# Where the attention output of a unit is summed: over the unit's q tile in place of its product buffer

## The chip, the cores and the metric

The kernel runs on one NeuronCore of a Trainium2 chip. The metric is the device time in microseconds (us) of one launch. Engines are named as in the profile: PE (TensorE, matrix products; PEld its weight loads), DVE (VectorE), ACT (ScalarE), POOL (GpSimd) and SP (SyncE, which here only issues DMAs). DMAs are issued from SP, ACT and POOL.

## The reference, cut to what matters

```python
xn = layernorm(x)                            # x: 2048 x 640, float32
q, k, v = split(xn @ wqkv)                   # 32 heads of 20
logits[s, w] = q[s] . k[s - 2*w] * 20**-0.5  # w = 0..7: a window of 8 rows, two apart; masked if s - 2*w < 0
o[s] = sum_w softmax(logits)[s, w] * v[s - 2*w]
s = o @ wo
h = (xn @ w_gate) * (xn @ w_up)              # 640 -> 1536
out = x + s * silu(h @ w_down)
```

## The kernel before

All matrix products are float32 work done as three products of high and low parts (`mm3` and `ALL3`), so a result tile of 512 columns takes 15 PE instructions. The work on PE has one order, written out by hand:

1. The rows are normalised and transposed.
2. Ten *units* follow. A unit is a group of 5, 6 or 7 heads (`GROUPS`) for the even or the odd rows (`DIL` = 2). Unit numbers 0, 2, 4, ... hold the even rows, 1, 3, 5, ... the odd ones. For each unit, `qkv(u, i)` computes eight row tiles (i = 0 to 7) in PE, each into one of four PSUM buffers with the tag `q`. ACT copies each result out: L317 the k and v part into the `kv` buffer of that parity (there is one for even and one for odd units), L318 the q part into the unit's q tile in SBUF (tag `q`, two buffers: unit u + 2 takes the buffer of unit u). L322 then shifts k and v by one partition with DMAs from ACT's queue, for the window.
3. Between units, PE computes four *pieces* of the feed-forward part (`gate_up`): a g product and a u product, each into one of two PSUM buffers (tags `g` and `u`). ACT copies g to SBUF (L423, `gs`), and DVE multiplies it with u (L434, `hs`). That frees the u buffer for the piece after the next.
4. The attention of a unit runs on DVE, as a generator (`attention(u)`) that `advance` moves on by a budget while PE works at the next unit or its pieces. So DVE's one queue holds the attention instructions with the L434s of the pieces between them. The order of each queue is fixed when the program is built.
5. After the units come the output projection and the down projection, which PE does without attention beside it.

Inside `attention(u)` a *pair tile* holds two of the eight window places, 2 x 800 to 2 x 1120 elements per partition. Pair tiles have the tag `t` and two buffers, which they take in turn: the products q times k (L351, `times`), their sums over the 20 elements of a head (L355, `total`), the exponential on ACT (L367), then the products of weights and v (L376) in one pair tile, `t`, added up into the other, `acc` (L384). Last, L387 adds the two halves of `acc`, and L392 stores the sum from SP to the scratch tensor `o_scr` in DRAM, in one DMA or two. The unit uses six pair tiles, an even number, so the second pair tile of the next unit's attention (the `times(2)` of L351) takes the buffer that was `acc`.

```python
for act, j in ((times, 0), (times, 2), (total, 0), (times, 4), (total, 2), (times, 6), (total, 4), (total, 6)):
```

Of the kernel before, what the change touches and what calls it, by code (L numbers as in the profile page):

```python
# [50 lines left out]
def kernel(  # L51
# [11 lines left out]
    nc = tc.nc  # L63
# [11 lines left out]
    def st(shape, tag, bufs, dt=F32):  # L75
        cnt[0] += 1
        return sb.tile(shape, dt, tag=tag, bufs=bufs, name=f"{tag}_{cnt[0]}")
# [248 lines left out]
    def attention(u):  # L326
        g, r = UN[u]
        nh = GROUPS[g]
        c = nh * DH
        q, kv = q_t[u], kv_t[u]  # L330
        pair, one, small = [(n + 155) / 950 for n in (2 * NE * c, NE * c, NE * nh * W)]
        lg = st([P, NE * nh, W], "lg", 2)
        e = lg
        yield 1.0

        def places(a, j):

            y = kv[:, a, j:j + NE, :].rearrange("p i c -> p (i c)")
            return bass.AP(y.tensor, y.offset, [y.ap[0], [c, 2], y.ap[1]])

        def pair_tile():
            return st([P, 2, NE * c], "t", 2)

        def heads(y):
            return y.rearrange("p a (n d) -> p a n d", d=DH)

        prods = {}

        def times(j):
            prods[j] = pair_tile()  # L350
            nc.vector.tensor_mul(prods[j], q.rearrange("p i c -> p (i c)").unsqueeze(1).to_broadcast([P, 2, NE * c]),  # L351
                                 places(0, j))

        def total(j):
            nc.vector.tensor_reduce(out=lg[:, :, j:j + 2].rearrange("p n a -> p a n"), in_=heads(prods.pop(j)),  # L355
                                    op=ALU.add, axis=AX.X)

        for act, j in ((times, 0), (times, 2), (total, 0), (times, 4), (total, 2), (times, 6), (total, 4), (total, 6)):
            act(j)
            yield pair  # L360
        m0 = lg[0:1].rearrange("p (i h) w -> p i h w", h=nh)
        nc.vector.tensor_add(m0, m0, mask.unsqueeze(2).to_broadcast([1, NE, nh, W]))
        sm = st([P, 2, NE * nh], "sm", 2)
        nc.vector.tensor_reduce(out=sm[:, 0, :], in_=lg, op=ALU.max, axis=AX.X)
        nc.vector.tensor_sub(lg, lg, sm[:, 0, :].unsqueeze(2).to_broadcast([P, NE * nh, W]))
        yield 3 * small
        nc.scalar.activation(e, lg, AF.Exp, scale=SCALE)  # L367
        yield small
        nc.vector.tensor_reduce(out=sm[:, 0, :], in_=e, op=ALU.add, axis=AX.X)
        nc.vector.reciprocal(sm[:, 1, :], sm[:, 0, :])  # L370
        nc.vector.tensor_mul(e, e, sm[:, 1, :].unsqueeze(2).to_broadcast([P, NE * nh, W]))
        yield 3 * small

        def weighted(j, t):
            pw = e[:, :, j:j + 2].rearrange("p n a -> p a n").unsqueeze(3).to_broadcast([P, 2, NE * nh, DH])
            nc.vector.tensor_mul(heads(t), pw, heads(places(1, j)))  # L376

        t, acc = pair_tile(), pair_tile()
        weighted(PAIRS[0], acc)
        yield pair  # L380
        for j in PAIRS[1:]:
            weighted(j, t)
            yield pair
            nc.vector.tensor_add(acc, acc, t)  # L384
            yield pair
        o = acc[:, 0, :].rearrange("p (i c) -> p i c", c=c)
        nc.vector.tensor_add(acc[:, 0, :], acc[:, 0, :], acc[:, 1, :])  # L387
        yield one
        for b in range(NQ):
            c0, c1 = max(GOFF[g], b * QC), min(GOFF[g] + c, (b + 1) * QC)  # L390
            if c0 < c1:
                nc.sync.dma_start(o_scr[r, b, :, :, c0 - b * QC:c1 - b * QC].rearrange("s p c -> p s c"),  # L392
                                  o[:, :, c0 - GOFF[g]:c1 - GOFF[g]])
# [328 lines left out]
    for i in range(8):  # L722
        if i == 3:
            running.append((0, attention(0)))
        if i == 2:
            load_wq(1, ((0, 3), (3, 5)))
            low_parts()
        if i < 2:
            trans_odd(14 + i)
        qkv(1, i)  # L730
        advance(PACE * 1.9)
    running.append((1, attention(1)))
    split_wq(1, nc.gpsimd)
    gate_up(0, 2)
# [19 lines left out]
    def unit(u):  # L754
        drain(u - 2)
        begin_unit(u)
        for i in range(NE):
            if u % 2 and u + 1 < len(UN) and i == 2:
                load_wq(UN[u + 1][0], ((0, 3), (3, 5)))
            qkv(u, i)  # L760
            if i == 1:
                finish_piece()
            advance(PACE * GROUPS[UN[u][0]] * 0.38)
        running.append((u, attention(u)))
        if u % 2 and u + 1 < len(UN):
            split_wq(UN[u + 1][0], nc.gpsimd)
# [127 lines left out]
```

## Time and profile before

| | |
|---|---|
| median of 3 runs | 778.89 us (778.88 to 779.15) |
| the profiled execution | 778.73 us, span of the trace 776.7 us |
| PE busy | 765.1 us, 99% of the span |
| DVE busy | 622.9 us, 80% |
| ACT busy | 250.9 us, 32% |
| POOL busy | 103.4 us, 13% |
| waits of DVE for the store to `o_scr`, at L351 | 18.9 us in 7 waits |
| waits of DVE for the shift of k and v, at L351 | 18.5 us in 6 waits |
| from issue to landing, 16 DMAs of L392 | 3.8 us least, 4.9 median, 8.8 most |

Busy time is the time in which an engine has an instruction of its own running. A row of a timeline gives start, duration, engine, line, operation, output and inputs (partitions x elements), and behind it in brackets how long the engine stood still before and what ended that. `xc`, `wf`, `wqh` and `wql` are the transposed rows and the weights; `lg` holds logits and weights of the window.

### The profile page before, as it was taken

The numbers are of one execution on the slowest core, as the hardware profiler recorded it, in microseconds if no ns is written. First come the engines' busy times: TensorE is split into PE (matmuls) and PEld (weight loads), VectorE is DVE, ScalarE is ACT, GpSimd is POOL, SyncE is SP. The second block draws the span as 40 slices with busy tenths as digits, with TensorE's granted clock in tenths as the row PEclk, the third lists the DMA queues.
The fourth block names the chain that finished last, engine by engine and source line by source line (L and its number), as shares of the span: only waits on it lengthen the run. The fifth ranks groups of instructions, "written<-read, shape, count | busy, mean of one in ns | idle before, by whom it ended". The sixth has DMA issues, their size and how long they took to land.

```text
span 776.7 us, 10632 instructions
## 1 busy us (share of the span) xinstructions
PE 765.1 (99%) x4214; PEld 704.9 (91%) x4214; DVE 622.9 (80%) x615; ACT 250.9 (32%) x519; POOL 103.4 (13%) x111
## 2 busy tenths in 40 slices
PE   8999999999899999999999999999999999999997
PEld 6989898897898989989889898888999999999997
DVE  6889889995989989699898898990277577777775
ACT  5333422132112241122412122112366554444442
POOL 5301110101001010000100000004387500000000
PEclk9999999999999999999999999999999999999999
DMA  9172441447133371433732413452897474555533
GB/s 330 62 233 84 90 117 45 96 147 129 34 93 87 113 169 47 104 86 111 147 71 80 111 31 112 109 159 75 190 270 211 160 265 169 193 188 184 183 103 136
DMA packets 82277, 103.33 MB, mean 133 GB/s; under 512 B 19036, under 2 KB 61376, under 8 KB 82100
## 3 DMA queue, kind: packets, MB, share of 16 engines
q1 hardware_dynamic: 72400, 82.85, 34.1%
q0 software_dynamic: 4128, 10.70, 8.3%
q10 hardware_dynamic: 5700, 9.11, 4.2%
q8 instruction: 33, 0.54, 0.3%
q14 instruction: 16, 0.13, 0.1%
HBM read 65.23 MB, written 28.31 MB: 120 GB/s over the span
## 4 chain that ended last, share of the span: by engine, by line
PE 83%; DVE 10%; DMA 4%; issue 2%; ACT 1%; SPq 0%; POOL 0%; DVEq 0%; POOLq 0%; ACTq 0%
PE q L315 21%; PE u L101 17%; PE g L101 16%; PE q L632 11%; PE q L101 9%; PE u L632 5%; PE g L632 3%; DVE t L376 3%; DVE lg L355 2%; DMA o_scr<-t 2%; DVE t L384 2%; DMA wraw<-in_wgu 1%; DVE t L351 1%; DVE hs L434 1%; DMA wraw<-in_wqkv 0%
## 5 line engine op out<-in xcount | busy, mean ns | idle before, releaser
L101 PE MATMUL u<-xc,wf 128*128 128x512 f32 (+1 forms) x735 | 173.5, 388 | 4.1 <-DVE hs L434 4.1
L101 PE MATMUL g<-xc,wf 128*128 128x512 f32 (+1 forms) x735 | 171.7, 385 | 0.0
L101 PEld LDWEIGHTS u<-xc,wf 128*128 128x128 f32 x735 | 137.1, 189 | 32.3 <-DVE hs L434 4.5
L101 PEld LDWEIGHTS g<-xc,wf 128*128 128x128 f32 x735 | 135.9, 188 | 26.6
L315 PE MATMUL q<-wqh,xc 128*128 128x420 f32 (+2 forms) x800 | 153.0, 334 | 1.6 <-ACT xc L244 0.9
L315 PEld LDWEIGHTS q<-wqh,xc 128*128 128x128 f32 x800 | 138.9, 188 | 3.4 <-ACT xc L244 1.3
L351 DVE TENSOR_TENSOR t<-q,kv 128x2240 f32<-128x2240 f32 (+2 forms) x40 | 91.2, 2287 | 37.6 <-DMA o_scr<-t 18.9
L376 DVE TENSOR_TENSOR t<-lg,kv 128x2240 f32<-128x2240 f32 (+2 forms) x40 | 90.8, 2290 | 0.9
L355 DVE TENSOR_REDUCE lg<-t 128x112 f32<-128x2240 f32 (+2 forms) x40 | 90.4, 2280 | 0.0
L423 ACT ACTIVATE gs<-g 128x512 f32<-128x512 f32 x48 | 28.6, 596 | 174.1 <-PE g L101 149.1
L315 PE MATMUL q<-wql,xc 128*128 128x420 f32 (+2 forms) x400 | 81.8, 334 | 0.0
L317 ACT ACTIVATE kv<-q 128x280 f32<-128x280 f32 (+2 forms) x80 | 30.6, 383 | 135.7 <-PE q L315 132.2
L315 PEld LDWEIGHTS q<-wql,xc 128*128 128x128 f32 x400 | 69.9, 188 | 0.0
L384 DVE TENSOR_TENSOR t<-t,t 128x2240 f32<-128x2240 f32 (+2 forms) x30 | 68.7, 2289 | 0.8
L632 PE MATMUL q<-xc,wf 128*128 128x320 f32 x432 | 67.3, 309 | 0.0
L632 PEld LDWEIGHTS q<-xc,wf 128*128 128x128 f32 x432 | 64.3, 188 | 0.0
L92 POOL DMA_DIRECT2D wf<-in_wgu x10 | 8.7, 873 | 283.9 <-ACT wf L91 277.9
L101 PE MATMUL q<-wf,wf 128*128 128x320 f32 x156 | 35.5, 309 | 0.0
L92 POOL DMA_DIRECT2D wql<-in_wqkv x8 | 10.2, 1281 | 131.6 <-ACT wql L91 131.0
L101 PEld LDWEIGHTS q<-wf,wf 128*128 128x128 f32 x156 | 26.1, 188 | 0.0
L434 DVE TENSOR_TENSOR hs<-u,gs 128x512 f32<-128x512 f32 x38 | 25.9, 682 | 0.0
L86 DVE TENSOR_TENSOR wf<-ot,wf 128x640 fp32r<-128x640 f32 x13 | 14.0, 1078 | 12.8 <-ACT wf L85 12.8
(167 smaller groups left out, 919.6 us busy)
## 6 DMA issues: line engine op xcount, KB each, us to landing
h_scr<-hs SPq DMA_DIRECT2D x48, 256.0 KB, 2.2
wraw<-in_wgu SPq DMA_DIRECT2D x12, 640.0 KB, 7.0
wf<-in_wgu POOLq DMA_DIRECT2D x10, 640.0 KB, 6.7
t<-h_scr SPq DMA_DIRECT2D x8, 768.0 KB, 7.1
hs<-s_scr SPq DMA_DIRECT2D x16, 320.0 KB, 4.3
gs<-in_x SPq DMA_DIRECT2D x16, 320.0 KB, 4.8
wraw<-h_scr SPq DMA_DIRECT2D x12, 384.0 KB, 6.3
out<-q SPq DMA_DIRECT2D x14, 320.0 KB, 3.8
```

The costliest lines, as they stand in the source:

```text
L86: eng.tensor_sub(lo, raw, hi.bitcast(F32))
L92: nc.gpsimd.dma_start(lo, src, accum_op=ALU.add)
L101: nc.tensor.matmul(acc, a, b, start=first and n == 0, stop=last and n == len(runs) - 1)
L315: nc.tensor.matmul(p, xT[(r * NE + i) // TPC][a][:, k, t0:t0 + P], wq[g][b][:, k], start=n == 0, stop=n == len(runs) - 1, skip_group_check ...
L317: nc.scalar.activation(kv_t[u][:, :, W - 1 + i, :], p[:, c:].rearrange("p (a c) -> p a c", a=2), AF.Copy)
L351: nc.vector.tensor_mul(prods[j], q.rearrange("p i c -> p (i c)").unsqueeze(1).to_broadcast([P, 2, NE * c]), places(0, j))
L355: nc.vector.tensor_reduce(out=lg[:, :, j:j + 2].rearrange("p n a -> p a n"), in_=heads(prods.pop(j)), op=ALU.add, axis=AX.X)
L376: nc.vector.tensor_mul(heads(t), pw, heads(places(1, j)))
L384: nc.vector.tensor_add(acc, acc, t)
L423: nc.scalar.activation(gs, pp[0], AF.Copy)
L434: nc.vector.tensor_mul(hs, pp[1], gs)
L632: nc.tensor.matmul(p, y[:, i, k], wd_t[name][k][:, l], start=new and r == 0, stop=r == len(runs) - 1, skip_group_check=True)
```

## The change

The last half-sum of a unit (L387) no longer overwrites the first half of `acc`; it is written over the unit's q tile, which the unit's attention has by then read for the last time (in `times(6)`). The store L392 reads it from there. Nothing else is edited.

```diff
-        o = acc[:, 0, :].rearrange("p (i c) -> p i c", c=c)
-        nc.vector.tensor_add(acc[:, 0, :], acc[:, 0, :], acc[:, 1, :])
+        o = q
+        nc.vector.tensor_add(o.rearrange("p i c -> p (i c)"), acc[:, 0, :], acc[:, 1, :])
         yield one
         for b in range(NQ):
             c0, c1 = max(GOFF[g], b * QC), min(GOFF[g] + c, (b + 1) * QC)
             if c0 < c1:
                 nc.sync.dma_start(o_scr[r, b, :, :, c0 - b * QC:c1 - b * QC].rearrange("s p c -> p s c"),
                                   o[:, :, c0 - GOFF[g]:c1 - GOFF[g]])
```

No engine's instructions change their number or their order. What changes is the waits, which the program's framework works out from who writes and reads each buffer.

On DVE, at the end of unit 2's attention and the start of unit 3's (`t_1584` is unit 2's `acc`, `q_1127` unit 2's q, `q_1472` unit 3's q; `DMAHW6` and the like count landings of DMAs on one of eight lanes):

```order
 L384 TENSOR_TENSOR t_1584<-t_1584,t_1583 128x1920 [waits DVE_49]
-L387 TENSOR_TENSOR t_1584<-t_1584 128x960 [waits DVE_49]
+L387 TENSOR_TENSOR q_1127<-t_1584 128x960 [waits DMAHW6_49,DVE_49]
 L434 TENSOR_TENSOR hs_1717<-u_1657,gs_1673 128x512 [waits DMAHW0_49,PE_49,Activation_49]
 L351 TENSOR_TENSOR t_1723<-q_1472,kv_109_763 128x1920 [waits DMAHW6_49,DMAHW5_49,DMAHW7_49,DMAHW0_49,Pool_49]
-L351 TENSOR_TENSOR t_1740<-q_1472,kv_109_763 128x1920 [waits DMAHW3_49,DMAHW2_49,DVE_49]
+L351 TENSOR_TENSOR t_1740<-q_1472,kv_109_763 128x1920 [waits DVE_49]
 L355 TENSOR_REDUCE lg_1722<-t_1723 128x2x48 [waits DVE_49]
 L434 TENSOR_TENSOR hs_1762<-u_1694,gs_1710 128x512 [waits DMAHW1_49,PE_49,Activation_49]
```

The second L351 of unit 3 no longer waits for the two DMAs of unit 2's store (lanes 2 and 3). The wait that L387 now names is for unit 0's store, from the buffer that unit 2's q later took.

On ACT, at the first row tile of unit 2, whose q takes the buffer of unit 0's q (`q_1129` and `q_1149` are PSUM results of PE, `q_1127` is the tile in SBUF):

```order
 L423 ACTIVATE gs_1101<-g_1084 128x512 [waits DVE_49,PE_49,Activation_49]
 L317 ACTIVATE kv_38_169<-q_1129 128x2x120 [waits DMAHW3_49,DMAHW4_49,DVE_49,PE_49]
-L318 ACTIVATE q_1127<-q_1129 128x120
+L318 ACTIVATE q_1127<-q_1129 128x120 [waits DMAHW6_49,DVE_49]
 L317 ACTIVATE kv_38_169<-q_1149 128x2x120 [waits PE_49]
 L318 ACTIVATE q_1127<-q_1149 128x120
```

The first L318 of a unit now waits for L387 and for the landing of the store two units before.

## The prediction

> **What bounds the kernel now.** I read the page's first part, then the waits of PE, the timeline of PE around its one wait, the granted clock there, and from there back into DVE. The page's busy times come first, then PE's waits from 100 us to the end:
>
> ```profile
> PE 765.1 (99%) x4214; PEld 704.9 (91%) x4214; DVE 622.9 (80%) x615; ACT 250.9 (32%) x519; POOL 103.4 (13%) x111
> ...
> PE u L101 <- DVE hs L434: 4.1, 1, 4.1
> ```
>
> PE is the bound: 99% busy, and once the units run it stands still once, for 4.1 us, for a DVE product L434. The timeline of PE shows what that stop costs, and the table of stretches gives the granted clock (the column of 1.00 and 0.68):
>
> ```profile
> 185.67 3.56 PE L101 MATMUL u<-xc,wf 128*128 128x512 f32 x15
> 189.07 3.56 PE L101 MATMUL g<-xc,wf 128*128 128x512 f32 x15
> 196.72 5.31 PE L101 MATMUL u<-xc,wf 128*128 128x512 f32 x15 [4.09 <-DVE hs L434]
> 201.87 1.10 PE L315 MATMUL q<-wqh,xc 128*128 128x420 f32 x5
> ...
> 192.63:196.72 4.09, 0.00 (x1) 0.00 (x1) 4.09 (x4) 0.00 (x0) 0.00 (x0) 1.00 0.00 0
> 196.72:200.20 3.48, 3.48 (x11) 2.77 (x12) 3.48 (x2) 0.60 (x1) 0.00 (x0) 0.68 0.26 78
> 200.20:202.03 1.83, 1.83 (x7) 1.46 (x6) 1.80 (x2) 0.00 (x0) 0.00 (x0) 0.68 0.00 0
> 202.03:224.43 22.40, 22.40 (x122) 22.40 (x121) 21.50 (x17) 4.47 (x15) 0.00 (x0) 1.00 0.17 50
> ```
>
> A product of 15 instructions starts 3.40 us after the one before (185.67 to 189.07). After the g of 189.07 the u was due at 192.47 and unit 4's q, k, v at 195.87; they began at 196.72 and 201.87. So the stop costs 201.87 - 195.87 = 6.00 us: 4.25 of lateness, and 1.75 more because the u itself took 5.15 us from start to start at a granted clock of 0.68. From 202.03 the clock is 1.00 again.
>
> Why L434 came late stands in DVE's timeline and in the chain of waits (SP issue, then the DMA from issue to landing):
>
> ```profile
> 178.87 3.56 PE L101 MATMUL u<-xc,wf 128*128 128x512 f32 x15
> ...
> 181.85 2.15 DVE L351 TENSOR_TENSOR t<-q,kv 128x1920 f32<-128x1920 f32 x1
> 191.85 2.16 DVE L351 TENSOR_TENSOR t<-q,kv 128x1920 f32<-128x1920 f32 x1 [7.85 <-DMA o_scr<-t]
> 193.92 2.15 DVE L355 TENSOR_REDUCE lg<-t 128x96 f32<-128x1920 f32 x1
> 195.99 0.68 DVE L434 TENSOR_TENSOR hs<-u,gs 128x512 f32<-128x512 f32 x1
> ...
> 182.39 0.50 SPq L392
> ...
> 182.94 8.78 DMA o_scr<-t
> ```
>
> The L434 of 195.99 multiplies the u that PE made from 178.87 and that was finished at 182.43. It came 13.5 us later because ahead of it in DVE's queue the second L351 of unit 3 stood 7.85 us for unit 2's store to land: the pair tile it writes was still being read by that DMA. PE's u buffer came free only with L434.
>
> **What the change removes.** The store reads the q tile, so no L351 has it to wait for. In all of DVE's waits:
>
> ```profile
> DVE t L351 <- DMA o_scr<-t: 18.9, 7, 7.8
> DVE t L351 <- DMA kv<-kv: 18.5, 6, 6.8
> ...
> 109.58 1.83 DVE L351 TENSOR_TENSOR t<-q,kv 128x1600 f32<-128x1600 f32 x1 [2.78 <-DMA o_scr<-t]
> ...
> 145.06 2.16 DVE L351 TENSOR_TENSOR t<-q,kv 128x1920 f32<-128x1920 f32 x1 [1.80 <-DMA o_scr<-t]
> ```
>
> At unit 3 the second L351 can follow the first at 181.85 + 2.15 = 184.00, which takes 7.85 us off the L434 as well: it starts at 188.14 and ends at 188.82, where PE wants the buffer at 192.47. That is 3.6 us to spare, without counting the lead of up to 2.78 + 1.80 us that units 1 and 2 gain earlier (ACT's exponential may take part of it back). The lateness was 4.25 us, so 3.6 us of new delay on DVE would have to appear before PE waits at all. The first term is therefore the whole 4.25 us.
>
> The second term is the 1.75 us at the reduced clock. While units run, the clock is below 1.00 only in the two stretches behind the one stop; otherwise only at the end, when PE has run dry:
>
> ```profile
> 105.00:192.00 87.00, 87.00 (x452) 78.33 (x452) 72.54 (x53) 22.00 (x49) 7.13 (x6) 1.00 0.46 109
> ...
> 202.00:554.00 352.00, 352.00 (x1682) 314.58 (x1681) 291.38 (x179) 81.51 (x168) 27.19 (x22) 1.00 0.40 100
> ...
> 772.40:776.70 4.30, 0.00 (x0) 0.00 (x0) 0.98 (x2) 0.34 (x1) 0.00 (x0) 0.78 0.21 76
> ```
>
> Both low clocks go with a PE that stands still for 4 us, so I take the dip to go with the stop. Bounds: 0 if the dip had another cause, 1.75 if it goes. I take 1.75, as nothing else in the middle of the trace pairs with a dip. The Trainium skill, "TensorE: Matmul & The Clock Gate", Part 1 (What's actually happening), says that PE falls to half rate after at least one idle window of about 3.4 us and gets the full rate back after a busy one; by that rule the gain is 6.00, by the stop alone 4.25, and the trace's order (4.09 us idle, then the lower clock) is as the rule has it.
>
> The other store waits that go (2.78, 1.80, 3.34 at 234.67 and three later that share the last 3.1 of the 18.9 us) never reached PE, which has only the one wait. They are worth nothing now: from unit 4 on, DVE starts each unit behind the landing of k and v, which PE's own progress sets.
>
> ```profile
> 228.83 2.49 DVE L351 TENSOR_TENSOR t<-q,kv 128x2240 f32<-128x2240 f32 x1 [0.24 <-DMA kv<-kv]
> 234.67 2.49 DVE L351 TENSOR_TENSOR t<-q,kv 128x2240 f32<-128x2240 f32 x1 [3.34 <-DMA o_scr<-t]
> ...
> 330.40 4.89 DVE L351 TENSOR_TENSOR t<-q,kv 128x2240 f32<-128x2240 f32 x2 [6.11 <-DMA kv<-kv]
> ```
>
> With PE 6.00 us earlier, the k and v of unit 4 land 6.00 us earlier, and DVE, freed before, waits for them some 3 to 4 us where it waited 0.24. Measured against PE, DVE is then as far as before at the first L351 and 3.34 us ahead at the second, so no L434 comes later than it did, and none of those stopped PE. The rest of the trace moves up as one piece.
>
> **What it adds.** L387 writes to another tile than it reads. The nearest rows are L351, which does too, and L384, which adds in place, both at 2240 elements:
>
> ```profile
> L351 DVE TENSOR_TENSOR t<-q,kv 128x2240 f32<-128x2240 f32 x24 | 59.5, 2486 | 25.0 <-DMA kv<-kv 18.5 <-DMA o_scr<-t 6.5
> L384 DVE TENSOR_TENSOR t<-t,t 128x2240 f32<-128x2240 f32 x18 | 44.8, 2489 | 0.4
> ```
>
> They differ by 3 ns, so ten L387 change by nothing, in either direction. Their new wait is for a store two units back, which has long landed. The DMAs of L392 keep number, sizes and place in SP's queue; only the source address differs.
>
> The price is a new wait on ACT: the first L318 of unit u + 2 waits for unit u's store. It is tight only where unit 2 follows unit 0:
>
> ```profile
> 105.09 4.01 DMA o_scr<-t
> ...
> 103.07 0.96 PE L315 MATMUL q<-wqh,xc 128*128 128x360 f32 x5
> ...
> 105.94 0.27 ACT L318 ACTIVATE q<-q 128x120 f32<-128x120 f32 x1
> 108.07 0.37 ACT L317 ACTIVATE kv<-q 128x240 f32<-128x240 f32 x1 [1.87 <-PE q L315]
> 110.47 0.37 ACT L317 ACTIVATE kv<-q 128x240 f32<-128x240 f32 x1 [1.87 <-PE q L315]
> ```
>
> The store lands at 109.10, and DVE's L351, which waited for the same landing, began 0.48 us behind it; so L318 goes from 105.94 to about 109.58. Behind it in ACT's queue are the copies of row tile 1 (108.07), which then run to about 110.5; tile 2 at 110.47 is on time within 0.1 us. PE is the one that waits for these copies: it has four PSUM buffers and needs tile 0's again for tile 4, at 103.07 + 4 x 2.40 = 112.67 (2.40 us is the spacing of 108.07 and 110.47). L318 is over by 109.85, 2.8 us before that. Hence nothing on the path. The bounds of this term: 0, and with the longest landing of an L392, 8.78, L318 would end at 105.09 + 8.78 + 0.48 + 0.27 = 114.62 and PE lose 1.95 us. I take 0, because the work up to 105 us is unchanged and 4.01 is this very store. The next pairs, units 1 and 3, 2 and 4, 3 and 5, have room:
>
> ```profile
> 140.62 4.35 DMA o_scr<-t
> ...
> 152.34 0.27 ACT L318 ACTIVATE q<-q 128x120 f32<-128x120 f32 x1
> ...
> 205.17 0.28 ACT L318 ACTIVATE q<-q 128x140 f32<-128x140 f32 x1
> ...
> 255.97 0.28 ACT L318 ACTIVATE q<-q 128x140 f32<-128x140 f32 x1
> ```
>
> Landing at 144.97 against 152.34 leaves 7.4 us. Unit 2's store lands at 191.72 at the latest, and unit 4's first L318 comes at about 199.2 once PE is 6.00 us earlier: 7.5 us. Unit 3's store had landed when the L351 of 234.67 began, 21 us ahead of unit 5's L318 at 255.97, and the later units have the same rhythm.
>
> The sum: 4.25 + 1.75 + 0 = 6.00 us, off the profiled execution's 778.73, gives 772.7 (span 776.7 to 770.7). The median of the runs is 0.16 above that execution, which makes 772.9. I write 772.8, 0.8% faster.
>
> **The rivals.**
> *The dip stays, or ACT's new wait shows on PE.* Either takes back up to 1.75 or 1.95 us: 774.5 or 774.7. For the second speaks that the wait lies on a queue that PE depends on, against it the 2.8 us to spare. The Trainium skill, same page, section on the array's architectural detail, calls ACT's queue strictly first in, first out, which speaks against the change: by it everything behind L318 waits too. The sum above has it so; were L318 passed by, even the 1.95 would be 0.
>
> *No gain: PE meets another wait at the same place.* The u buffer's L434 also stands behind unit 3's first L351, which needs k and v of unit 3, and behind L355. If something there held DVE 7.85 us, as the store did, the time would stay 778.9. Against it: that L351 began at 181.85 without waiting, so its k and v had landed by then, and whatever lead the queue gains or loses up to there, L434 is not later than 188.14.
>
> *Slower, through L318.* If the store of unit 0 landed so late that PE's wait for tile 0's buffer outgrew the gain: it waits (landing - 6.83) us, so break-even is a landing of 12.8 us after issue, and 14.4 gives 780.3. No L392 took more than 8.78.
>
> *Faster than 772.3.* It would need PE time that the trace does not show as waiting after 100 us; I give it little.
>
> **How the numbers follow.** Full gain 0.80 (772.3 to 773.2); part of it, 773.2 to 775.5, 0.08; no gain 0.06; slower 0.03; still faster 0.03. The range from 772.2 to 774.8 takes in the full gain, the bound without the dip (774.5) and that with the longest landing (774.7). A measurement here tells about 0.2%, 1.6 us, from no change: faster 0.90, same 0.07, slower 0.03.
>
> **What would show it.** Right: PE's 4.1 us wait for L434 gone, and no clock under 1.00 between 20 and 765 us; no wait of L351 for the store; waits of L351 for k and v longer than 18.5 us in sum; one hold of about 3.6 us on ACT at the first L318 of unit 2, with no PE wait at the fifth row tile; L387 at its old durations. Wrong: a PE wait for ACT's L317 or L318 anywhere, an L387 that grew, or a new stop of PE at 192 us with another name behind it.

## The result, and the profile after

| | before | after |
|---|---|---|
| median | 779.02 us (778.88 to 780.5, 4 runs) | 772.94 us (772.57 to 773.06, 4 runs) |
| the profiled execution | 778.73 us, span 776.7 | 772.99 us, span 771.0 |

The ratio is 0.9917, with a 95% interval of 0.9900 to 0.9934: 6.1 us less, where 6.0 and a time of 772.8 us were forecast. The waits of PE in the whole profile of after:

```profile
PE q L171 <- POOL lg masks.py:199: 1.4, 1, 1.4
PE q L315 <- DVE xc L245: 1.2, 1, 1.2
PE q L315 <- ACT xc L244: 0.9, 2, 0.6
```

All of them belong to the start (transposes and first products); the stop of 4.1 us for L434 is gone, and nothing has come in its place. The same stretch of PE's timeline as before, with the granted clock (the last column but two) of the u product and of unit 4's q, k, v:

```profile
189.40 3.56 PE L101 MATMUL g<-xc,wf 128*128 128x512 f32 x15
192.79 3.56 PE L101 MATMUL u<-xc,wf 128*128 128x512 f32 x15
196.19 1.09 PE L315 MATMUL q<-wqh,xc 128*128 128x420 f32 x5
...
192.79:196.19 3.40, 3.40 (x16) 2.81 (x15) 3.40 (x3) 0.60 (x1) 0.00 (x0) 1.00 0.26 80
196.19:218.59 22.40, 22.40 (x121) 22.39 (x120) 20.63 (x16) 4.49 (x15) 0.00 (x0) 1.00 0.13 38
```

From the g to unit 4's first product PE takes 196.19 - 189.40 = 6.79 us, before 201.87 - 189.07 = 12.80: 6.01 us less. (The spans differ by 5.7 because this execution's first steps ran about 0.3 us later; this shift is in all times of after.) In DVE's timeline, the two first L351 of unit 3 now follow each other in one row:

```profile
177.47 1.16 DVE L387 TENSOR_TENSOR q<-t 128x960 f32<-128x960 f32 x1
179.14 4.22 DVE L351 TENSOR_TENSOR t<-q,kv 128x1920 f32<-128x1920 f32 x2
183.28 2.15 DVE L355 TENSOR_REDUCE lg<-t 128x96 f32<-128x1920 f32 x1
185.34 0.68 DVE L434 TENSOR_TENSOR hs<-u,gs 128x512 f32<-128x512 f32 x1
...
DVE t L351 <- DMA kv<-kv: 28.6, 6, 8.5
```

L434 starts at 185.34 where it stood at 195.99, and is over at 186.02, 6.8 us before PE needs the buffer (192.79). DVE got no less waiting by that: its waits for k and v grew from 18.5 to 28.6 us, since it now runs ahead and waits for what PE makes. In the longest of them, 8.5 us at unit 4, k and v also came late; the part on why the prediction was right takes that up. The new wait on ACT shows at the place forecast:

```profile
109.05 0.27 ACT L318 ACTIVATE q<-q 128x120 f32<-128x120 f32 x1 [2.69 <-DMA o_scr<-q]
109.22 0.37 ACT L317 ACTIVATE kv<-q 128x240 f32<-128x240 f32 x1
110.79 0.37 ACT L317 ACTIVATE kv<-q 128x240 f32<-128x240 f32 x1 [1.05 <-PE q L315]
```

ACT stands 2.69 us for unit 0's store, copies row tile 1 right behind it, and is waiting for PE again at tile 2. PE never waited for it.

### The profile page after: what moved, and what is told of

Same layout as the page of the kernel before. It is cut to its first block, busy times and chain, and to the rows that moved or that the text cites. A ratio compares the mean times of both kernels' runs of the same rounds, so it can differ in the third digit from the quotient of the medians.

```text
span 771.0 us, 10626 instructions
## 1 busy us (share of the span) xinstructions
PE 763.1 (99%) x4214; PEld 703.7 (91%) x4214; DVE 622.4 (81%) x615; ACT 251.2 (33%) x519; POOL 103.0 (13%) x111
## 4 chain that ended last, share of the span: by engine, by line
PE 97%; DMA 2%; ACT 0%; POOL 0%; DVE 0%; issue 0%; SPq 0%; POOLq 0%
PE q L315 26%; PE u L101 21%; PE g L101 21%; PE q L632 11%; PE q L101 9%; PE u L632 5%; PE g L632 3%; DMA wraw<-in_wgu 1%; DMA wraw<-in_wqkv 1%; PE q L243 0%; POOL wql L86 0%; ACT wf L85 0%; SPq L148 0%; PE q L263 0%; DVE xc L245 0%
## 5 line engine op out<-in xcount | busy, mean ns | idle before, releaser
L351 DVE TENSOR_TENSOR t<-q,kv 128x2240 f32<-128x2240 f32 (+2 forms) x40 | 90.6, 2286 | 28.8 <-DMA kv<-kv 28.6
L423 ACT ACTIVATE gs<-g 128x512 f32<-128x512 f32 x48 | 28.6, 596 | 174.0 <-PE g L101 164.9
L92 POOL DMA_DIRECT2D wql<-in_wqkv x8 | 10.2, 1281 | 133.1 <-ACT wql L91 132.5
L434 DVE TENSOR_TENSOR hs<-u,gs 128x512 f32<-128x512 f32 x38 | 25.9, 683 | 0.0
```

The lines of the kernel that those rows point to most:

```text
L92: nc.gpsimd.dma_start(lo, src, accum_op=ALU.add)
L423: nc.scalar.activation(gs, pp[0], AF.Copy)
L434: nc.vector.tensor_mul(hs, pp[1], gs)
```

## The experiments

Where an edit adds lines, the numbers of the lines below it are a few higher in that kernel: L438 and L435 are L434, L352 is L351, L388 is L387.

### One unit alone

```diff
+        if u == 2:
             o = q
             nc.vector.tensor_add(o.rearrange("p i c -> p (i c)"), acc[:, 0, :], acc[:, 1, :])
+        else:
+            o = acc[:, 0, :].rearrange("p (i c) -> p i c", c=c)
+            nc.vector.tensor_add(acc[:, 0, :], acc[:, 0, :], acc[:, 1, :])
```

> The new place for the half-sum is used in unit 2 alone; the other nine units add and store as before. Theory (the gain is the one stop of PE behind unit 2's store): the whole gain, 772.9 us, no PE wait after 100 us and no clock under 1.00 there; DVE still waits for the stores of the other units, 18.9 - 7.85 = about 11 us in six waits. Rival (the gain is spread over the units' store waits, 18.9 us in seven): 7.85 of 18.9 of it, 2.5 us, so 776.4.

This run is `unit2_only`: 773.23 us (772.55 to 773.58), ratio 0.9914 (0.9895 to 0.9933) to the kernel before on the same chip: the whole gain. PE has no wait after 100 us, the granted clock is 1.00 over the whole run, and waits of DVE for stores are still there, 8.9 us where some 11 were expected:

```profile
DVE t L351 <- DMA kv<-kv: 22.2, 6, 6.5
DVE t L351 <- DMA o_scr<-t: 8.9, 5, 2.6
```

So one of the ten places is enough for the whole result, and beside it the nine others cost and bring nothing on PE.

### The store of unit 2 made twice as long

In the kernel before, unit 2's store is issued twice to the same place; the second waits for the first to land.

```diff
-        for b in range(NQ):
+        for b in range(2 * NQ if u == 2 else NQ):
+            b %= NQ
```

> The kernel before, with unit 2's store issued twice to the same place, each DMA waiting for the landing of its first. Theory: the second L351 of unit 3 waits for the second landing, 4 to 5 us later (nothing else moves data by then), and PE's stop of 4.1 us grows by as much, to 8 to 9 us; the time grows by 4 to 5 us, and by up to 1.7 more if the longer stop brings a second window of the lower clock: 783 to 785.7. Rival (the stop has another cause than this store's landing): 778.9 to 779.5.

`store2_twice`: 786.15 us (783.44 to 786.69), ratio 1.0078 (1.0064 to 1.0091): 6.1 us slower than the kernel before on that chip (780.07), where the range expected was 4.1 to 6.8 us above 778.9; the time itself lies 0.5 us above it. The chain has the two landings, and PE's timeline and the granted clock the longer stop:

```profile
182.69 9.90 DMA o_scr<-t
192.60 3.41 DMA o_scr<-t
...
201.01 5.88 PE L101 MATMUL u<-xc,wf 128*128 128x512 f32 x15 [8.30 <-DVE hs L435]
206.73 1.10 PE L315 MATMUL q<-wqh,xc 128*128 128x420 f32 x5
...
195.50:201.01 5.51, 0.00 (x1) 0.00 (x1) 4.87 (x4) 0.00 (x0) 0.00 (x0) 0.50 0.00 0
201.01:206.73 5.72, 5.72 (x16) 4.58 (x16) 5.69 (x3) 0.60 (x1) 0.00 (x0) 0.59 0.16 47
```

The stop went from 4.09 to 8.30 us, and the u behind it took 5.72 us from start to start (5.15 before, 3.40 at full clock). These two account for 4.8 us. The execution that was profiled is the fastest of the five (783.44); what the others took beyond that, 2.7 us at the median, no trace shows.

### All units but unit 2, and unit 1 alone

The same `if` with `u != 2` and with `u == 1`.

> The new place is used in all units but unit 2. Theory: DVE reaches unit 2's end some 3.0 us earlier than before (in the profile of after, L387 of unit 2 stands at 177.47 where before, shifted by the 0.32 us later start, it was 180.49), its store from the pair tile lands some 8.1 us after 180.4, and PE stops for only 0.5 to 1.3 us. If the lower clock comes only with a stop of about 4 us, the time is 773.4 to 774.2; if it comes with any stop, 1.75 more, 775.2 to 776. Rival (the gain is spread over the units): 11 of 18.9 of 6 us, 3.5 us, so 775.4, with a stop of PE as long as before.

> The new place is used in unit 1 alone, so that only the 1.80 us wait at unit 2's second L351 goes. Theory: PE's stop shrinks from 4.25 us of lateness by 1.80 to about 2.45. With the lower clock tied to a stop of 4 us the time is 778.9 - 1.80 - 1.75 = 775.4; with the lower clock at any stop 777.1. Rival (a wait of DVE that PE does not see is worth nothing): 778.9.

All but unit 2 (`all_but_unit2`): 773.98 us (773.23 to 774.56), ratio 0.9923 (0.9906 to 0.9941), as expected without the lower clock. DVE came to unit 2's end about 3 us earlier, and the stop shrank to 1.47 us, with a granted clock of 1.00 behind it (0.5 to 1.3 us were expected, but the store took 9.06 us to land and not 8.1):

```profile
189.38 2.16 DVE L351 TENSOR_TENSOR t<-q,kv 128x1920 f32<-128x1920 f32 x1 [8.26 <-DMA o_scr<-t]
...
194.26 3.69 PE L101 MATMUL u<-xc,wf 128*128 128x512 f32 x15 [1.47 <-DVE hs L438]
...
194.26:197.79 3.53, 3.53 (x15) 2.92 (x16) 3.53 (x2) 0.60 (x1) 0.00 (x0) 1.00 0.26 77
```

The wait at unit 3's second L351 is as long as ever (8.26 us); it only begins earlier. So the gain has nothing to do with how much waiting DVE does, only with when L434 is over. The nine other places, which bring nothing beside unit 2's, bring 5.4 us (779.40 to 773.98) without it.

Unit 1 alone (`unit1_only`): 775.01 us (774.76 to 776.77), ratio 0.9941 (0.9923 to 0.9959), near the 775.4 expected, but not by the sum that I gave:

```profile
193.63 3.70 PE L101 MATMUL u<-xc,wf 128*128 128x512 f32 x15 [0.53 <-DVE hs L438]
...
237.45 3.69 PE L101 MATMUL u<-xc,wf 128*128 128x512 f32 x15 [0.73 <-DVE hs L438]
```

The first stop shrank by more than the 1.80 us expected, to 0.53 us: unit 2's store, issued earlier, landed in 7.48 us and not in 8.78, and in this execution DVE stood only 2.32 us for unit 0's store, not 2.78. And a second stop appeared at 237.45: with PE earlier, the wait for unit 3's store (3.34 us before, 4.01 here), which had never reached PE, now did.

### Why just unit 2's store

In the profile of before it lands 8.78 us after issue, the longest of all. At 182.36 us POOL issues a 640 KB accumulating DMA for the weights of column 4. In this variant of the kernel before, their low parts are made by five subtractions on POOL.

```diff
-        if f > 1:
+        if f > 1 and f != 4:
             split_dma(wf_raw[f], wgu[f], hi, lo)
         else:
+            cuts = range(KD + 1) if f == 4 else cuts
             for k0, k1 in zip(cuts, cuts[1:]):
                 split(eng, wf_raw[f][:, k0:k1], hi[:, k0:k1], lo[:, k0:k1])
```

> The kernel before, with the low parts of the weights of feed-forward column 4 made by POOL with five subtractions and not by the 640 KB accumulating DMA that POOL issues at 182.36 us, beside unit 2's store. Theory (that store alone stopped PE because it landed only 8.8 us after issue, beside this load, where the others took 4 to 6): it lands in 4 to 6 us, PE's lateness falls from 4.25 to 0.3 to 1.5 us without the lower clock, 773.2 to 774.5. Rival (the store is slow for its two DMAs or for the weight loads issued before it): a landing of 7 to 9 us, the stop and the time stay, 777 to 779.

`no_load_beside_store2`: 775.6 us (774.36 to 776.13), ratio 0.9943 (0.993 to 0.9955). From the chain, and the waits of PE:

```profile
183.90 5.30 DMA o_scr<-t
...
194.20 3.71 PE L101 MATMUL u<-xc,wf 128*128 128x512 f32 x15 [1.22 <-DVE hs L435]
...
238.44 3.69 PE L101 MATMUL u<-xc,wf 128*128 128x512 f32 x15 [1.13 <-DVE hs L435]
```

The load was what made the store slow: without it the store lands in 5.30 us, PE stops for 1.22 us, the clock stays at 1.00. (With the load, and the store from the pair tile, the chains of five traces show 7.48 to 9.90 us.) The time is 1.1 us above my range: again unit 3's store became a second stop, 1.13 us at 238.44, which I had not counted.

### The two pair tiles exchanged: not the test it was meant to be

```diff
-        t, acc = pair_tile(), pair_tile()
+        acc, t = pair_tile(), pair_tile()
```

> The kernel before, with the two pair tiles of the weighted sum taken in the other order (acc first, then t), so that the first L351 of the next unit has to wait for the store and no longer the second. Everything is computed as before. Theory: every store wait on DVE grows by the length of one L351, 1.8 to 2.5 us; three such waits stand ahead of the stop of PE, so L434 comes 4 to 6 us later and PE's lateness at unit 3 is 7 to 10 us in place of 4.25: 781 to 785, with further short stops possible at unit 4. Rival (which buffer the store reads does not matter to PE): 778.9.

`sum_tile_first`: 779.55 us (777.45 to 783.05), ratio 1.0006 (0.999 to 1.0021). DVE's timeline shows that it still is the second L351 that waits:

```profile
181.33 2.15 DVE L351 TENSOR_TENSOR t<-q,kv 128x1920 f32<-128x1920 f32 x1
191.65 2.16 DVE L351 TENSOR_TENSOR t<-q,kv 128x1920 f32<-128x1920 f32 x1 [8.17 <-DMA o_scr<-t]
```

The framework gives a new tile the buffer that came free first, and that of `t` is always free before that of `acc`, whichever was taken first. So the edit moved no wait, and the statement ahead of the prediction that the pair tiles take their buffers in turn is wrong; which L351 waits was right. The run says nothing for or against the rival; store2_twice took its place.

### The new wait on ACT, made longer

In the kernel after, unit 0's store is issued two and three times, as with unit 2's above (`2 * NQ if u == 0` and `3 * NQ if u == 0`).

> The kernel after, with unit 0's store issued twice to the same place, the second waiting for the landing of the first. Theory (the first L318 of unit 2 holds PE only when it ends past about 113.0 us): the second landing is at 112.8 to 113.5, L318 ends 0.3 to 0.8 us later, PE stops for 0 to 1.3 us: 772.9 to 774.3, no lower clock. Rival (ACT's hold costs PE as much as it lasts): some 7 us of hold, 779 or more.

> The kernel after, with unit 0's store issued three times, each waiting for the landing of the one before. Theory: the third landing is at 116.6 to 118, L318 ends at 117 to 118.5, PE stops at about 113.0 for 4 to 5.5 us, and a stop of that length brings the lower clock with it: 772.9 + 4 to 5.5 + 1.75 = 778.7 to 780.2. If the lower clock has to do with the place at 197 us and not with a stop: 776.9 to 778.4. Rival (ACT's hold is hidden whatever its length): 772.9.

Twice (`store0_twice`): 774.59 us (774.33 to 774.94), ratio 0.9934 (0.9917 to 0.9951). Three times (`store0_thrice`): 780.06 us (779.05 to 781.01), ratio 1.0004 (0.9992 to 1.0015). ACT's first L318 and PE's fifth row tile, for twice, then for three times, there with the granted clock:

```profile
114.11 0.27 ACT L318 ACTIVATE q<-q 128x120 f32<-128x120 f32 x1 [7.71 <-DMA o_scr<-q]
112.23 0.96 PE L315 MATMUL q<-wqh,xc 128*128 128x360 f32 x5
114.44 1.09 PE L315 MATMUL q<-wqh,xc 128*128 128x360 f32 x5 [1.25 <-ACT q L318]
...
117.10 0.27 ACT L318 ACTIVATE q<-q 128x120 f32<-128x120 f32 x1 [10.84 <-DMA o_scr<-q]
112.09 0.96 PE L315 MATMUL q<-wqh,xc 128*128 128x360 f32 x5
117.42 1.87 PE L315 MATMUL q<-wqh,xc 128*128 128x360 f32 x5 [4.37 <-ACT q L318]
...
113.05:115.45 2.40, 0.01 (x1) 0.00 (x0) 2.37 (x2) 0.00 (x0) 0.00 (x0) 0.99 0.74 204
115.45:117.42 1.97, 0.00 (x0) 0.00 (x0) 1.97 (x2) 0.32 (x2) 0.00 (x0) 0.50 1.08 266
117.42:122.25 4.83, 4.83 (x16) 4.83 (x17) 4.03 (x5) 1.23 (x6) 0.00 (x0) 0.50 0.16 65
```

A hold of 7.71 us on ACT costs PE 1.25 us, one of 10.84 us costs 4.37: PE pays only what lies beyond the fifth row tile, as forecast. With three stores the whole gain of the change is gone. The first of the two is 0.3 us above its range: the two landings took 8.5 us together, not 7.4 to 8.0, and the four row tiles after the stop (114.44 to the next g at 124.41) took 9.97 us where 4 x 2.40 were due. I have no row that explains these 0.37 us.

## Why the prediction was right

- **The stop at unit 3 is the whole gain.** The first term, 4.25 us, held: the stop went, PE needs 6.79 us for what took 12.80, unit 2 alone gives all of it, and a longer store there makes the kernel slower. L434 was over 3.1 us earlier than forecast (at 186.02, where 188.82 and the shift of 0.3 us make 189.1), by the lead of units 1 and 2 that the sum had left out.
- **The lower clock goes with the stop.** The second term, 1.75 us, was chosen by two coincidences in one trace. The runs carry it: with stops of 0.5 to 1.5 us (unit1_only, all_but_unit2, no_load_beside_store2, store0_twice) the clock stayed at 1.00; with 4.1 us and more (before, sum_tile_first, store0_thrice, store2_twice) it fell to 0.50. In store0_thrice the dip moved with the stop, from 198 us to 115 us, and the clock from 190 to 205 us was 1.00. The size is less fixed than the term had it: 1.75 us in this execution, 2.3 (5.72 - 3.40) in store2_twice. No run has a stop between 1.5 and 4.1 us, so where between them the dip begins is open.
- **The other store waits are worth nothing.** This holds beside unit 2's place, as unit2_only shows, but the reason given, that they never reached PE, is wrong. The waits of 2.78 and 1.80 us stand ahead of the stop in DVE's one queue and made L434 later: without the 1.80 alone the kernel gains 4.4 us (779.40 to 775.01, unit1_only, part of it from stores that landed sooner there). And unit 3's wait stays away from PE only as long as PE is late: with the stop mended by another way than the change, it cost 0.73 and 1.13 us. That the change took all store waits away at once kept both from showing.
- **The rest of the trace does not move up as one piece.** The forecast had k and v of unit 4 land 6.00 us earlier, so that no L434 came later against PE. In the kernel after, they let DVE go at 227.25, only 1.6 us earlier than the 228.83 of before. Rows of after, then the L434 and the u product of before:

```profile
218.82 0.99 SPq L392 DMA_DIRECT2D o_scr<-q  x2
219.91 0.58 SPq L131 DMA_DIRECT2D wraw<-in_wgu  x1
219.23 1.58 ACTq L322 DMA_DIRECT2D kv<-kv  x2
227.25 4.89 DVE L351 TENSOR_TENSOR t<-q,kv 128x2240 f32<-128x2240 f32 x2 [8.50 <-DMA kv<-kv]
234.46 0.68 DVE L434 TENSOR_TENSOR hs<-u,gs 128x512 f32<-128x512 f32 x1
235.59 3.56 PE L101 MATMUL u<-xc,wf 128*128 128x512 f32 x15
...
239.47 0.68 DVE L434 TENSOR_TENSOR hs<-u,gs 128x512 f32<-128x512 f32 x1
241.27 3.56 PE L101 MATMUL u<-xc,wf 128*128 128x512 f32 x15
```

  The shift of k and v (L322) is now issued within a microsecond of unit 3's store, which the earlier DVE brought forward, and of a 640 KB weight load; its last two DMAs took 6.2 and 7.1 us to land, where they took 3.6 and 3.0 in the kernel before, with the store and the load 3 us and more behind them. That the store and the load slowed it is likely, but no run tests it. L434 was over at 235.14, 0.45 us before PE wanted the buffer; before it was 1.12 us. So the rest of the gain held by half a microsecond, which the forecast had not seen: in that it was lucky.
- **ACT's wait is hidden.** It was forecast at 3.6 us and measured at 2.69, since the store landed by 109.0, some 3.5 us after its issue, not 4.01, and L318 began about 0.1 us behind the landing, not 0.48. No PE wait, as forecast. The rule for the rival, (landing - 6.83) us, gives 1.70 for the landing at 114.01 of store0_twice (8.53 after its issue at 105.48), where PE was 1.41 late (due at 112.23 + 0.80, restarted at 114.44); it is 0.3 too high, mainly because L318 began 0.10 us behind the landing, not 0.48 as DVE's L351 had.
- **L387 out of place costs nothing.** For 960 elements it took 1.16 us before and takes 1.16 now.
- **DVE runs into k and v.** Forecast as waits above 18.5 us in sum; they are 28.6. At unit 4, 3 to 4 us were forecast and 8.50 measured, as above.

## What to carry to other kernels

Where a result is stored from decides what the transfer holds up, so store from the buffer whose next writer is furthest away: here q, next written 8 us or more after the store lands except at one place, in place of a product buffer that was wanted two or three instructions later. Of a stall on an engine that is not the bound, only the part counts that reaches the bound: look for the one wait of PE and follow it back, and price a new wait by the slack at its tightest place. After mending one stop, look which wait is next in line; two of these variants met it 44 us on. And look what the transfers of the engine that now runs earlier will run beside.

## What the runs showed of the hardware that I had not expected

- The lower clock can begin before PE has stood still for 3.4 us: in store0_thrice the granted clock was 0.99 in the 2.40 us after the stop began and 0.50 from then on, and in store2_twice it fell 2.8 us after the stop began (192.71 to 195.50), while in the kernel before it fell only about 1.2 us after PE had started again (rows below). The low stretches have lengths near 3.4 us and its multiples: about 3.4 us before, 1.97 + 4.83 = 6.8 in store0_thrice, about 10.2 in store2_twice. The Trainium skill, "TensorE: Matmul & The Clock Gate", Part 1, gives an idle window of about 3.4 us on a free-running grid. The lengths fit whole windows; the need for a whole idle one does not, in store0_thrice and store2_twice. (The profile models the ends of PE's instructions, so the start of a stop is not exact.)

```profile
196.72:197.90 1.18, 1.18 (x5) 1.00 (x6) 1.18 (x1) 0.60 (x1) 0.00 (x0) 1.00 0.27 79
198.05:201.30 3.25, 3.25 (x9) 2.58 (x8) 3.22 (x3) 0.00 (x0) 0.00 (x0) 0.50 0.13 39
```

- The kernels with the long stop scatter more: 777.5 to 781.6 us for the kernel before on a second chip, against 772.6 to 773.6 for unit2_only there. The record has the mean granted clock of every execution. Of 43 executions of the kernel before on three chips, the 20 with 0.997 or more have a median of 778.8 us, the 23 with less one of 780.6; all six of unit2_only have 1.000. So more time at the lower clock goes with the longer times, though not on each chip (among the 9 executions on one of them no relation shows), and where the low stretches lie only a profiled execution shows.
- DVE beside POOL: L387 of 960 elements, 1.16 us elsewhere, took 1.58 us while POOL subtracted in no_load_beside_store2. The two DVE instructions right behind it, with POOL still at work, took their usual 0.68 and 2.14 us, so what made the one longer is open.

```profile
180.71 1.58 DVE L388 TENSOR_TENSOR t<-t 128x960 f32<-128x960 f32 x1
...
180.42 6.52 POOL L86 TENSOR_TENSOR wf<-wraw,wf 128x256 fp32r<-128x256 f32 x5 [3.61 <-ACT wf L85]
```
